# A fourth raw-weight buffer, stores held back by one weight, and four columns begun on half of their tokens

## The chip, the cores and the metric

The kernel runs on one core of a Trainium2 chip. The metric is device time in microseconds (us) of one execution, the median of several runs; lower is better.

## What is computed

Attention with a memory term, then two feed-forward networks (FFNs), in float32 (B=4, H=8, S=576, D=64, model width 512, inner width 2048):

```
a = softmax(causal(q k^T / 8));  local = a v
mem = (phi(q) M_prev) / (phi(q) z_prev + 1e-6);  g = sigmoid(beta)
x = g * mem + (1 - g) * local          # 4 x 576 tokens x 512
x = softplus(x W1in) W1out             # first FFN ("layer 0")
x = elu(x W2in) W2out                  # second FFN ("layer 1")
```

The weights arrive as float64, viewed as pairs of 32-bit words.

## The kernel before

**Tokens.** The 2304 tokens are cut into five chunks (`CHUNKS`). Chunk 0 is tokens 0 to 255 of batches 0 and 1, so its 512 columns are batch 0's half (columns 0 to 255, `CA` = 256) and batch 1's half. Each chunk goes through layer 0 and then layer 1.

**Weights.** A weight tile is 128x4x128: `0i3` is column block 3 of layer 0's input matrix, `1o2_1` is piece 1 of output block 2 of layer 1. Every matrix has 16 such tiles. The first time, a tile is loaded raw (512 KB, `raw`, into a buffer of the tag `big`), turned into float32 on ACT and DVE (`convert`: L606 on ACT, L607 and L608 on DVE), and split into a high part (L97 on ACT) and a low part (L618 on DVE) in one of the four `w` buffers of the pool `wp`. It is also stored to a scratch tensor in DRAM (`save`, L583, 512 KB), from which the later chunks reload it (L656). The tag `big` has three buffers, which the attention's raw head tiles (`load_head`) share. All loads and stores of weights go through SP's queue, which is in order: a store that waits for its conversion holds up the load behind it.

**FFN.** A column block `f` of an input product is 12 matmuls into one PSUM bank `h`: for each of four k blocks (128 of the 512 inputs, two heads' pair of the attention) high x high, high x low and low x high (L690 to L692). Then come the activation and a split into `g` (L665 to L696, on ACT and DVE), which free the bank. There are four `h` banks (`psf`), and the early attention of batches 0 and 1 uses the same four for its scores (L371, `bank`). An output product has 16 pieces of 12 matmuls (L707 to L709).

**Attention.** The early part ("A") of batches 0 and 1 runs first. `gather_pair` writes one k block of `x` for one batch (L150, L151); its last matmul is kept in `marks`. The rest (A of batches 2 and 3, then the late part "B" of all four batches) is cut into steps, which `order` in `TUNE` mixes into the FFN: an entry `(chunk, layer, a, b)` means `a` steps for each of the 16 column blocks and `b` steps for each of the 16 output pieces.

**Order.** A scheduler sets each engine's order when the program is built; each engine then works in order. Fourteen of the first matrix's 16 tiles are converted before chunk 0 starts. So in layer 1 of chunk 0 (184 to 310 us of the span, below "the w2i stage" and "the w2o stage") every weight is loaded raw, converted, used and stored for the first time.

Of the kernel before, what the change touches and what calls it, by code (L numbers as in the profile page):

```python
# [8 lines left out]
F32 = mybir.dt.float32  # L9
# [4 lines left out]
I32 = mybir.dt.int32  # L14
# [3 lines left out]
NP = H // 2  # L18
KD = DM // 128
# [6 lines left out]
CA = 256  # L26
# [13 lines left out]
    hi='ssss ssss', lo='v', sc='vv ssv',  # L40


    order=((0, 0, 0.95, 0.95), (0, 1, 0.25, 1.0), (1, 0, 0.45, 1.6), (1, 1, 0.4, 0.9), (2, 0, 0.3, 0.8), (2, 1, 0.4, 0.7), (3, 0, 0.3, 0.8), (3, 1, 0.4, 0.7), (4, 0, 0.0, 0.0), (4, 1, 0.0, 0.0)),
)


# [12 lines left out]
def kernel(  # L59
# [20 lines left out]
    four = ctx.enter_context(tc.tile_pool(name="four", bufs=4))  # L80
    tri = ctx.enter_context(tc.tile_pool(name="tri", bufs=3))
    wp = ctx.enter_context(tc.tile_pool(name="wp", bufs=4))
    gp = ctx.enter_context(tc.tile_pool(name="gp", bufs=KF))
    dram = ctx.enter_context(tc.tile_pool(name="dram", bufs=1, space=bass.MemoryType.DRAM))
    psf = ctx.enter_context(tc.tile_pool(name="psf", bufs=4, space=bass.MemoryType.PSUM))
# [49 lines left out]
    def x(c, k):  # L135
        return slots[SLOT[c]][k]
# [5 lines left out]
    gates, column, marks = [], [], {}  # L142
# [11 lines left out]
    def attention(b, part, pool, early=None):  # L154
# [15 lines left out]
        def own(h):  # L170
            return slice(64 * h, 64 * h + 64)
# [12 lines left out]
            d["kq", p] = t  # L184

        def load_head(n):
            t = tri.tile([128, 960], F32, name="qk", tag="big")
            if n % 2:
                at = S + QO[4]
                ge.dma_start(t[:, 0:at], qk[b, n, :, 0:at])  # L190
                ge.dma_start(t[:, at:at + 64], qk[b, n, :, at + 64:at + 128])
                ge.dma_start(t[:, at + 64:at + 128], qk[b, n, :, at:at + 64])
            else:
                ge.dma_start(t, qk[b, n, :, 0:960])
            d["qk", n] = t
# [169 lines left out]
        def scores_pair(n):  # L365
            p, ps = n // 2, [bank(n), bank(n + 1)]
            for i in (1, 0):
                w_, at = width(i), poff(0, i)
                for h in range(2):
                    t, q0 = d["kq", p], CA + 128 * i  # L370
                    te.matmul(ps[h][:, at:at + w_], t[own(h), q0:q0 + 128], t[own(h), 0:w_], start=True, stop=True)  # L371
            for h in range(2):
                P, neg = sph[h], d["neg", n + h]
                for i in (1, 0):
                    w_, at, to = width(i), poff(0, i), poff(n, i)
                    negmax(P[:, to:to + w_], ps[h][:, at:at + w_], mask[:, 512 - w_:512], neg[:, i:i + 1])
                    expo(n + h, i)
# [213 lines left out]
            fetched[key] = raw(w1i[f])  # L591

    def raw(src):
        w64 = tri.tile([128, 4, 128, 2], I32, name="w64", tag="big")
        load = nc.sync.dma_start(w64.rearrange("p k n t -> p (k n t)"), src.bitcast(I32))
        raw_loads.append(load.ins)
        sync.append(load.ins)
        return w64

    def convert(src, key, w=None):  # L600
        wr = tri.tile([128, 4, 128], F32, name="wr", tag="wr")
        if wide:
            w64 = fetched.pop(key) if key in fetched else raw(src)
            low, high = w64[:, :, :, 0], w64[:, :, :, 1]
            wi = wr.bitcast(I32)
            se.activation(wr, high.bitcast(F32), ACTF.Prelu, scale=2.0 ** -112, alpha=-(2.0 ** 32))  # L606
            ve.tensor_scalar(wi, wi, 3, None, ALU.logical_shift_left)  # L607
            ve.scalar_tensor_tensor(wi, low, 29, wi, ALU.logical_shift_right, ALU.bitwise_or)  # L608
        else:
            w64 = tri.tile([128, 4, 128, 2], I32, name="w64", tag="big")  # L610
            load = nc.sync.dma_start(wr.rearrange("p k n -> p (k n)"), src)
            raw_loads.append(load.ins)
            sync.append(load.ins)
        if w is None:
            w = w64.rearrange("p k n t -> p (k n t)").rearrange("p (s k n) -> p s k n", s=2, k=4).bitcast(F32R)
        hi, lo = w[:, 0], w[:, 1]
        copy(E[T["hi"].split()["o" in key][int(key[0])]], hi, wr)
        E[T["lo"]].tensor_sub(lo, wr, f32(hi))  # L618
        return w
# [3 lines left out]
    def weights(src, key):  # L623
        if key in made:
            w = made.pop(key)
            unsaved.append((key, w))
        else:
            early = key.startswith("0i") and key not in scratch
            with tc.high_priority(offset=T["pri"][key in scratch]), tc.issue_after(softs[int(key[2:]) - 10]) if early else nullcontext():
                new = key not in scratch  # L630
                passes[key] = passes.get(key, 0) + 1
                w = make(src, key)
            if len(raw_loads) >= KF:
                with tc.issue_after(sync[-1]):
                    while unsaved:
                        save(*unsaved.pop(0))
            with tc.issue_after(sync[-1]):
                put()
            if new and not (key in twice and passes[key] == 1):
                unsaved.append((key, w))  # L640
        return w[:, 0], w[:, 1]
# [11 lines left out]
    def make(src, key, pool=None):  # L653
        w = (pool or wp).tile([128, 2, 4, 128], F32R, name="w", tag="g" if pool else "w")
        if key in scratch:
            sync.append(nc.sync.dma_start(f32(w), scratch[key]).ins)  # L656
        else:
            convert(src, key, w)
        return w
# [3 lines left out]
    def act(c, layer, f, t, h):  # L663
# [9 lines left out]
        else:  # L673
            ve.tensor_scalar(t, h, 0.0, None, ALU.min)
            se.activation(t, t, ACTF.Exp)
            ve.scalar_tensor_tensor(t, t, -1.0, h, ALU.add, ALU.max)  # L676

    def ffn(c, layer):
        win, wout = ((w1i, w1o), (w2i, w2o))[layer]
        N = WIDTH[c]  # L680
        gs = []
        for f in range(KF):
            hi, lo = weights(win[f], f"{layer}i{f}")
            t = two.tile([128, 512], F32, name="t", tag="t")
            g = gp.tile([128, 2, 512], F32R, name="g", tag="g")
            h = psf.tile([128, 512], F32, name="h", tag="h")
            with tc.issue_after(marks[1, NP - 1][0]) if (c, layer) == (0, 0) and f < 4 else nullcontext():
                for k in range(KD):
                    xk = x(c, k)
                    te.matmul(h[:, :N], hi[:, k, :], xk[:, 0, :N], start=k == 0, stop=False)  # L690
                    te.matmul(h[:, :N], hi[:, k, :], xk[:, 1, :N], start=False, stop=False)  # L691
                    end = te.matmul(h[:, :N], lo[:, k, :], xk[:, 0, :N], start=False, stop=k == KD - 1)  # L692
            column[:] = [end.ins]
            act(c, layer, f, t[:, :N], h[:, :N])
            se.copy(g[:, 0, :N], t[:, :N])  # L695
            ve.tensor_sub(g[:, 1, :N], t[:, :N], f32(g)[:, 0, :N])  # L696
            gs.append(g)
            if layer and f == KF - 1:
                busy[c].add("in")
            yield  # L700
        for d in range(KD):
            h = psf.tile([128, 512], F32, name="h", tag="h")
            for u in range(4):
                hi, lo = weights(wout[d, u], f"{layer}o{d}_{u}")
                for k in range(4):
                    f = 4 * u + k
                    te.matmul(h[:, :N], hi[:, k, :], gs[f][:, 0, :N], start=f == 0, stop=False)  # L707
                    te.matmul(h[:, :N], hi[:, k, :], gs[f][:, 1, :N], start=False, stop=False)  # L708
                    end = te.matmul(h[:, :N], lo[:, k, :], gs[f][:, 0, :N], start=False, stop=f == KF - 1)  # L709
                column[:] = [end.ins]  # L710
                if u < 3:
                    yield
            if layer == 0:
                y = x(c, d)
                se.copy(y[:, 0, :N], h[:, :N])
                ve.tensor_sub(y[:, 1, :N], h[:, :N], f32(y)[:, 0, :N])
            else:
                o = two.tile([128, 512], F32, name="t", tag="t")
                copy(se, o[:, :N], h[:, :N])
                outs.append((c, d, o))  # L720
                if c == len(CHUNKS) - 1:
                    put()
            yield
# [36 lines left out]
    with tc.tile_pool(name="pre", bufs=1) as pre, tc.tile_pool(name="pre3", bufs=2) as pre3:  # L760
# [12 lines left out]
        with tc.issue_after(marks[1, NP - 2][1]), tc.issue_after(marks[1, NP - 2][2]):  # L773
            while len(made) < count:
                key = f"0i{len(made)}"
                made[key] = make(w1i[len(made)], key)
    late = ctx.enter_context(tc.tile_pool(name="late", bufs=1))
    slots.append([late.tile([128, 2, WIDTH[2]], F32R, name=f"x2_{k}") for k in range(KD)])

# [100 lines left out]
```

## Time and profile before

| | us |
|---|---|
| median of 3 runs (1055.76 to 1058.61) | 1056.13 |
| the profiled execution | 1053.93 |
| its span, first to last instruction | 1052.1 |

The profile is of one execution, so its parts add up to the span and not to the median. PE is TensorE's matmuls, PEld its weight loads, DVE is VectorE, ACT is ScalarE, SP issues the weight transfers, POOL the attention's. An engine's row shows when an instruction began, how long it took and, in brackets, how long the engine had stood before it and what released it.

### The profile page before, as it was taken

The page shows a single profiled execution, that of the slowest core. Times are in us where ns is not written, and L with a number is a line of the kernel's source. Part 1 is how long each engine was busy: PE and PEld are TensorE (multiplying, and loading weights), DVE is VectorE, ACT ScalarE, POOL GpSimd, SP SyncE. Part 2 cuts the span into 40 slices and gives each one's busy share as a digit, 9 for nine tenths or more (in the row PEclk, how much of TensorE's full clock was granted, in tenths as well). Part 3 has the DMA queues.
Part 4 walks back from the last instruction along what each step waited for, and adds up shares of the span by engine and source line. Part 5 has one row for each costly group of instructions (what it writes and reads, how often), then busy time and mean ns, then how long its engine had stood idle before and what let it go on. Part 6 is the DMA issues. An engine that isn't in the chain of part 4 may idle for free.

```text
span 1052.1 us, 15858 instructions
## 1 busy us (share of the span) xinstructions
PE 1011.3 (96%) x5249; PEld 897.7 (85%) x5249; DVE 672.3 (64%) x1701; ACT 664.5 (63%) x1518; POOL 104.0 (10%) x198
## 2 busy tenths in 40 slices
PE   6699999978989999999999999999999999999998
PEld 4477777767868888888889899999999999999998
DVE  6958887887768665798666667854665570240640
ACT  5869865877669955787679756555885440570420
POOL 7121221020111011000110011000000000000000
PEclk9899999999999999999999999999999999999999
DMA  8558888975786466566775666666755567777675
GB/s 245 166 207 311 288 293 299 336 264 197 232 288 223 160 203 203 177 221 227 259 245 184 223 221 215 191 233 213 234 189 172 175 233 243 251 235 233 235 238 171
DMA packets 71185, 240.27 MB, mean 228 GB/s; under 512 B 10288, under 2 KB 15552, under 8 KB 71104
## 3 DMA queue, kind: packets, MB, share of 16 engines
q1 hardware_dynamic: 62272, 207.65, 58.2%
q0 software_dynamic: 8832, 31.61, 9.8%
q8 instruction: 42, 0.69, 0.3%
q14 instruction: 39, 0.32, 0.1%
HBM read 200.95 MB, written 38.27 MB: 227 GB/s over the span
## 4 chain that ended last, share of the span: by engine, by line
PE 77%; DVE 8%; DMA 6%; ACT 5%; issue 3%; SPq 0%; ACTq 0%; DVEq 0%
PE h L707 12%; PE h L709 12%; PE h L708 12%; PE h L690 10%; PE h L692 10%; PE h L691 10%; DMA w<-in_w2o 3%; PE tp L409 3%; PE o L456 2%; PE s L343 2%; DMA w<-in_w2i 1%; PE s L355 1%; DVE wr L608 1%; DVE w L618 1%; DVE sph L332 1%
## 5 line engine op out<-in xcount | busy, mean ns | idle before, releaser
L690 PE MATMUL h<-x,w 128*128 128x512 f32 (+2 forms) x640 | 240.7, 378 | 8.3 <-DVE t L672 7.4
L707 PE MATMUL h<-g,w 128*128 128x512 f32 (+2 forms) x640 | 241.7, 378 | 0.3 <-ACT w L97 0.2
L709 PE MATMUL h<-g,w 128*128 128x512 f32 (+2 forms) x640 | 239.2, 374 | 0.5 <-DVE w L618 0.5
L708 PE MATMUL h<-g,w 128*128 128x512 f32 (+2 forms) x640 | 238.9, 373 | 0.0
L692 PE MATMUL h<-x,w 128*128 128x512 f32 (+2 forms) x640 | 238.3, 373 | 0.0
L691 PE MATMUL h<-x,w 128*128 128x512 f32 (+2 forms) x640 | 238.3, 373 | 0.0
L690 PEld LDWEIGHTS h<-x,w 128*128 128x128 f32 x640 | 120.9, 189 | 24.5 <-DVE t L672 9.4
L709 PEld LDWEIGHTS h<-g,w 128*128 128x128 f32 x640 | 121.2, 189 | 13.2 <-DVE w L618 1.1
L707 PEld LDWEIGHTS h<-g,w 128*128 128x128 f32 x640 | 121.2, 189 | 13.1 <-ACT w L97 0.7
L692 PEld LDWEIGHTS h<-x,w 128*128 128x128 f32 x640 | 120.7, 189 | 13.7 <-issue 0.2
L691 PEld LDWEIGHTS h<-x,w 128*128 128x128 f32 x640 | 121.0, 189 | 12.0
L708 PEld LDWEIGHTS h<-g,w 128*128 128x128 f32 x640 | 121.3, 190 | 10.9
L696 DVE TENSOR_TENSOR g<-t,g 128x512 fp32r<-128x512 f32 (+2 forms) x160 | 100.9, 634 | 32.2 <-ACT g L695 30.6
L695 ACT CAST g<-t 128x512 fp32r<-128x512 f32 (+2 forms) x160 | 91.5, 574 | 33.2 <-DVE t L676 25.8
L336 ACT ACTIVATE sph<-sph,neg 128x256 f32<-128x256 f32 (+4 forms) x144 | 83.4, 580 | 32.2 <-DVE neg L332 32.0
L668 DVE SCALAR_TENSOR_TENSOR t<-h,t 128x512 f32<-128x512 f32 (+2 forms) x80 | 50.3, 635 | 65.0 <-ACT t L667 64.6
L332 DVE CUSTOM_DVE_ANT_0 sph<-s,mask 128x256 f32<-128x256 f32 (+3 forms) x112 | 56.0, 520 | 49.4 <-PE s L343 41.9
L606 ACT ACTIVATE wr<-w 128x512 f32<-128x512 f32 x70 | 46.7, 672 | 36.9 <-DMA w<-in_w2o 16.3
L409 PE MATMUL tp<-ident,sph 128*128 128x128 f32 x400 | 61.6, 278 | 8.3 <-DVE sph L385 3.6
L409 PEld LDWEIGHTS tp<-ident,sph 128*128 128x128 f32 x400 | 48.9, 144 | 16.1 <-DVE sph L385 3.9
L420 DVE TENSOR_TENSOR ptj<-tp,ptj 128x512 fp32r<-128x512 f32 (+2 forms) x80 | 40.1, 513 | 31.8 <-ACT ptj L419 25.2
L97 ACT COPY t<-h 128x512 f32<-128x512 f32 (+2 forms) x20 | 10.8, 542 | 74.4 <-PE h L709 74.3
(134 smaller groups left out, 1498.8 us busy)
## 6 DMA issues: line engine op xcount, KB each, us to landing
w<-s_0i SPq DMA_DIRECT2D x64, 512.0 KB, 4.2
w<-s_0o SPq DMA_DIRECT2D x64, 512.0 KB, 3.3
w<-s_1i SPq DMA_DIRECT2D x62, 512.0 KB, 3.5
w<-s_1o SPq DMA_DIRECT2D x60, 512.0 KB, 4.1
w<-in_w2o SPq DMA_DIRECT2D x20, 512.0 KB, 4.6
w<-in_w2i SPq DMA_DIRECT2D x18, 512.0 KB, 5.5
w<-in_w1i SPq DMA_DIRECT2D x16, 512.0 KB, 4.9
s_0i<-w SPq DMA_DIRECT2D x16, 512.0 KB, 10.5
```

The source lines that it names most:

```text
L332: ve.tensor_tensor_reduce(out=dst, in0=ps, in1=m, scale=-0.125, scalar=least, op0=ALU.add, op1=ALU.min, accum_out=acc)
L336: se.activation(Pi, Pi, ACTF.Exp, scale=-1.0, bias=d["neg", n][:, i:i + 1], accum_out=sums(n, i))
L409: te.transpose(pt, sph[n % 2][:, poff(n, i) + 128 * j:poff(n, i) + 128 * j + 128], ident)
L668: ve.scalar_tensor_tensor(t, h, 0.0, t, ALU.max, ALU.add)
L690: te.matmul(h[:, :N], hi[:, k, :], xk[:, 0, :N], start=k == 0, stop=False)
L691: te.matmul(h[:, :N], hi[:, k, :], xk[:, 1, :N], start=False, stop=False)
L692: end = te.matmul(h[:, :N], lo[:, k, :], xk[:, 0, :N], start=False, stop=k == KD - 1)
L695: se.copy(g[:, 0, :N], t[:, :N])
L696: ve.tensor_sub(g[:, 1, :N], t[:, :N], f32(g)[:, 0, :N])
L707: te.matmul(h[:, :N], hi[:, k, :], gs[f][:, 0, :N], start=f == 0, stop=False)
L708: te.matmul(h[:, :N], hi[:, k, :], gs[f][:, 1, :N], start=False, stop=False)
L709: end = te.matmul(h[:, :N], lo[:, k, :], gs[f][:, 0, :N], start=False, stop=f == KF - 1)
```

## The change

Four edits. The tag `big` moves to a pool of its own with four buffers. While layer 1's weights are first converted, `weights` leaves one tile unsaved, so that each store is issued one weight later. The steps of attention per FFN piece are shifted: chunk 0's layer 0 takes 32 steps instead of 30.4, the output pieces of its layer 1 take 12 instead of 16, and those of chunk 1's layer 0 take 28 instead of 25.6. And `open_columns` begins column blocks 0 to 3 of chunk 0 on batch 0's half and the first two k blocks, behind batch 1's last scores and batch 0's third gather; `ffn` later does the other half of these k blocks.

```diff
-    order=((0, 0, 0.95, 0.95), (0, 1, 0.25, 1.0), (1, 0, 0.45, 1.6), ...
+    order=((0, 0, 1.0, 1.0), (0, 1, 0.25, 0.75), (1, 0, 0.45, 1.75), ...
...
+    big = ctx.enter_context(tc.tile_pool(name="big", bufs=4))
...
-            t = tri.tile([128, 960], F32, name="qk", tag="big")
+            t = big.tile([128, 960], F32, name="qk", tag="big")
...
-                    te.matmul(ps[h][:, at:at + w_], t[own(h), q0:q0 + 128], t[own(h), 0:w_], start=True, stop=True)
+                    done = te.matmul(ps[h][:, at:at + w_], t[own(h), q0:q0 + 128], t[own(h), 0:w_], start=True, stop=True).ins
+            marks[b, p, "s"] = done
...
-        w64 = tri.tile([128, 4, 128, 2], I32, name="w64", tag="big")
+        w64 = big.tile([128, 4, 128, 2], I32, name="w64", tag="big")
...
-                    while unsaved:
+                    while len(unsaved) > (new and key[0] == "1"):
                         save(*unsaved.pop(0))
...
+    def product(h, hi, lo, c, k, a, z):
+        xk = x(c, k)
+        te.matmul(h[:, a:z], hi[:, k, :], xk[:, 0, a:z], start=k == a == 0, stop=False)
+        te.matmul(h[:, a:z], hi[:, k, :], xk[:, 1, a:z], start=False, stop=False)
+        return te.matmul(h[:, a:z], lo[:, k, :], xk[:, 0, a:z], start=False, stop=k == KD - 1)
+
+    starts = {}
+
+    def open_columns():
+        for f in range(4):
+            starts[f] = (*weights(w1i[f], f"0i{f}"), psf.tile([128, 512], F32, name="h", tag="h"))
+        for k, behind in enumerate((marks[1, NP - 1, "s"], marks[0, 2][0])):
+            with tc.high_priority(offset=2000), tc.issue_after(behind):
+                for hi, lo, h in starts.values():
+                    product(h, hi, lo, 0, k, 0, CA)
+
     def ffn(c, layer):
...
-            hi, lo = weights(win[f], f"{layer}i{f}")
+            begun = (c, layer) == (0, 0) and f in starts
+            hi, lo = starts[f][:2] if begun else weights(win[f], f"{layer}i{f}")
...
-            h = psf.tile([128, 512], F32, name="h", tag="h")
-            with tc.issue_after(marks[1, NP - 1][0]) if (c, layer) == (0, 0) and f < 4 else nullcontext():
+            h = starts[f][2] if begun else psf.tile([128, 512], F32, name="h", tag="h")
+            with tc.issue_after(marks[1, NP - 1][0]) if begun else nullcontext():
                 for k in range(KD):
-                    xk = x(c, k)
-                    te.matmul(h[:, :N], hi[:, k, :], xk[:, 0, :N], start=k == 0, stop=False)
-                    te.matmul(h[:, :N], hi[:, k, :], xk[:, 1, :N], start=False, stop=False)
-                    end = te.matmul(h[:, :N], lo[:, k, :], xk[:, 0, :N], start=False, stop=k == KD - 1)
+                    end = product(h, hi, lo, c, k, CA if begun and k < 2 else 0, N)
...
+        open_columns()
```

PE's order behind batch 0's third gather (`o_400`, pair 2), before. `tp_467` is the memory product of the next pair.

```order
L472 MATMUL o_400<-ident_89,e_263 128x128 x2
L475 MATMUL o_400<-pt_346,ar0_2_147 64x256
L475 MATMUL o_400<-pt_347,ar0_2_147 64x256
L475 MATMUL o_400<-pt_346,ar0_2_147 64x128
L475 MATMUL o_400<-pt_347,ar0_2_147 64x128
L287 MATMUL tp_467<-mz_421,phi_443 128x130 x2
```

The same place now (the gather is `o_403`; `h_768` and `h_769` are column blocks 0 and 1, `x0_0` and `x0_1` the first two k blocks).

```order
L477 MATMUL o_403<-pt_349,ar0_2_150 64x128
L477 MATMUL o_403<-pt_350,ar0_2_150 64x128
L682 MATMUL h_768<-x0_0_100,w_209 128x256
L683 MATMUL h_768<-x0_0_100,w_209 128x256
L684 MATMUL h_768<-x0_0_100,w_209 128x256
L682 MATMUL h_768<-x0_1_101,w_209 128x256
L683 MATMUL h_768<-x0_1_101,w_209 128x256
L684 MATMUL h_768<-x0_1_101,w_209 128x256
L682 MATMUL h_769<-x0_0_100,w_250 128x256
L683 MATMUL h_769<-x0_0_100,w_250 128x256
L684 MATMUL h_769<-x0_0_100,w_250 128x256
```

With block 1's three for the second k block, which follow, twelve matmuls of 256 columns stand between the gather and the next memory product (`tp_470` now). Blocks 2 and 3 stand in the same way behind batch 0's fourth gather.

SP's order at the beginning of layer 1's output matrix, before. `w64_2653` is the raw tile of `1o0_2`, whose converted tile is `w_2651`.

```order
L595 DMA w64_2653<-in_w2o 128x1024
L583 DMA s_1o0_0_2624<-w_2541 128x1024
L595 DMA w64_2688<-in_w2o 128x1024
L595 DMA w64_2738<-in_w2o 128x1024
L583 DMA s_1o0_2_2695<-w_2651 128x1024
L583 DMA s_1o0_3_2745<-w_2686 128x1024
L595 DMA w64_2795<-in_w2o 128x1024
L583 DMA s_1o1_0_2802<-w_2736 128x1024
L595 DMA w64_2838<-in_w2o 128x1024
```

The same place now. The raw tile of `1o0_2` is `w64_2692`, its converted tile `w_2690`.

```order
L597 DMA w64_2692<-in_w2o 128x1024
L585 DMA s_1i14_2662<-w_2556 128x1024
L597 DMA w64_2737<-in_w2o 128x1024
L585 DMA s_1o0_0_2744<-w_2632 128x1024
L597 DMA w64_2795<-in_w2o 128x1024
L597 DMA w64_2820<-in_w2o 128x1024
L585 DMA s_1o0_2_2802<-w_2690 128x1024
L597 DMA w64_2863<-in_w2o 128x1024
L585 DMA s_1o0_3_2827<-w_2735 128x1024
```

The store of `1o0_2` stands behind two later loads before and behind three now, that of `1o0_3` behind one before and three now.

## Rows read from the trace of the kernel before

**Rows 1.** The page: the span, and PE's busy time.

```profile
span 1052.1 us, 15858 instructions
...
PE 1011.3 (96%) x5249; PEld 897.7 (85%) x5249; DVE 672.3 (64%) x1701; ACT 664.5 (63%) x1518; POOL 104.0 (10%) x198
```

**Rows 2.** Windows: busy us by engine, granted clock, DMA share, GB/s.

```profile
0.00:60.00 60.00, 41.64 (x215) 30.39 (x215) 45.28 (x190) 40.91 (x125) 24.25 (x52) 0.94 0.62 183
60.00:184.00 124.00, 122.65 (x610) 95.36 (x611) 99.49 (x281) 93.63 (x219) 25.49 (x46) 1.00 0.84 295
184.00:235.00 51.00, 43.58 (x186) 33.72 (x185) 42.62 (x78) 41.39 (x76) 6.48 (x12) 0.97 0.85 299
235.00:310.00 75.00, 67.41 (x330) 55.34 (x329) 58.46 (x145) 51.59 (x118) 9.15 (x18) 0.95 0.70 236
310.00:1000.00 690.00, 688.24 (x3661) 635.59 (x3660) 415.63 (x989) 427.84 (x965) 38.63 (x70) 1.00 0.65 216
```

**Rows 3.** PE's timeline at the stalls of both stages.

```profile
212.13 0.50 PE L690 MATMUL h<-x,w 128*128 128x512 f32 x1 [2.65 <-DVE t L672]
...
212.93 0.39 PE L690 MATMUL h<-x,w 128*128 128x512 f32 x1
...
217.60 0.40 PE L692 MATMUL h<-x,w 128*128 128x512 f32 x1
...
228.03 0.80 PE L690 MATMUL h<-x,w 128*128 128x512 f32 x1 [3.97 <-DVE t L672]
...
231.15 0.40 PE L691 MATMUL h<-x,w 128*128 128x512 f32 x1
...
263.57 0.66 PE L409 MATMUL tp<-ident,sph 128*128 128x128 f32 x4 [3.25 <-DVE ptj L420]
...
265.23 0.80 PE L707 MATMUL h<-g,w 128*128 128x512 f32 x1 [0.21 <-ACT w L97]
...
268.74 0.40 PE L709 MATMUL h<-g,w 128*128 128x512 f32 x1
...
294.29 0.77 PE L409 MATMUL tp<-ident,sph 128*128 128x128 f32 x5 [3.62 <-DVE sph L385]
```

**Rows 4.** ACT's timeline ahead of PE's stall that ends at 228.03.

```profile
217.97 0.99 ACT L97 CAST R<-qk 128x960 fp32r<-128x960 f32 x1 [1.42 <-DMA qk<-in_qk]
...
222.97 0.67 ACT L606 ACTIVATE wr<-w 128x512 f32<-128x512 f32 x1 [1.39 <-DMA w<-in_w2o]
```

**Rows 5.** ACT's longest wait, 184 to 310: us in total, times, longest.

```profile
ACT wr L606 <- DMA w<-in_w2o: 11.3, 11, 1.5
```

**Rows 6.** SP's waits, 184 to 310: us in total, times, longest.

```profile
SPq L595 <- DVE wr L608: 28.8, 15, 3.4
SPq L583 <- DVE w L618: 23.9, 15, 4.1
```

**Rows 7.** Landing times of w2o's 16 loads, by tile.

```profile
DMA to landing us min/median/max: 3.4/4.6/5.9
```

**Rows 8.** Landing times of 14 of the stores of w2i, by tile.

```profile
DMA to landing us min/median/max: 3.3/4.8/7.4
```

**Rows 9.** PE's timeline in the early attention, after two of batch 0's gathers.

```profile
45.08 0.69 PE L287 MATMUL tp<-mz,phi 128*128 128x130 f32 x4 [1.46 <-issue]
...
49.43 0.68 PE L287 MATMUL tp<-mz,phi 128*128 128x130 f32 x4 [1.42 <-DVE phi L263]
```

**Rows 10.** DVE's timeline: the last reads of two score banks.

```profile
44.24 0.29 DVE L332 CUSTOM_DVE_ANT_0 sph<-h,mask 128x128 f32<-128x128 f32 x1
...
48.65 0.29 DVE L332 CUSTOM_DVE_ANT_0 sph<-h,mask 128x128 f32<-128x128 f32 x1
```

**Rows 11.** PE's timeline: two matmuls of 256 columns, and the next.

```profile
282.21 0.39 PE L458 MATMUL o<-ptl,vs 128*128 128x256 f32 x2
282.45 0.33 PE L459 MATMUL o<-sph,vs 128*128 128x64 f32 x2
```

**Rows 12.** The page: the weight loads of L690, mean ns of one.

```profile
L690 PEld LDWEIGHTS h<-x,w 128*128 128x128 f32 x640 | 120.9, 189 | 24.5 <-DVE t L672 9.4
```

More of the change, by code (lines that the diff above doesn't have):

```diff
@@ L40 @@
     hi='ssss ssss', lo='v', sc='vv ssv',
-    order=((0, 0, 0.95, 0.95), (0, 1, 0.25, 1.0), (1, 0, 0.45, 1.6), (1, 1, 0.4, 0.9), (2, 0, 0.3, 0.8), (2, 1, 0.4, 0.7), (3, 0, 0.3, 0.8), (3, 1, 0.4, 0.7), (4, 0, 0.0, 0.0), (4, 1, 0.0, 0.0)),
+    order=((0, 0, 1.0, 1.0), (0, 1, 0.25, 0.75), (1, 0, 0.45, 1.75), (1, 1, 0.4, 0.9), (2, 0, 0.3, 0.8), (2, 1, 0.4, 0.7), (3, 0, 0.3, 0.8), (3, 1, 0.4, 0.7), (4, 0, 0.0, 0.0), (4, 1, 0.0, 0.0)),
 )
@@ L609, in convert @@
         else:
-            w64 = tri.tile([128, 4, 128, 2], I32, name="w64", tag="big")
+            w64 = big.tile([128, 4, 128, 2], I32, name="w64", tag="big")
             load = nc.sync.dma_start(wr.rearrange("p k n -> p (k n)"), src)
```

## The prediction

> **What bounds the kernel now.** I read the page's first part, then windows over the whole span, then PE's timeline where the windows show PE standing, then the waits of ACT and SP in that stretch. PE is busy 1011.3 of 1052.1 us [rows 1], so time can only come from the 40.8 us in which PE stands, from matmuls that run at the lower clock, or from fewer matmul columns. The windows say where PE stands: 18.4 us in the first 60 us, 1.4 us up to 184, 7.4 us in the w2i stage, 7.6 us in the w2o stage, 1.8 us in the 690 us after that, and the rest at the end [rows 2]. Nothing in the change touches the last two.
>
> In the two stages the granted clock is 0.97 and 0.95 as well [rows 2]. PE's timeline shows how: after standing 3.97 us it goes on at 228.03, and the seven matmuls up to 231.15 take 3.12 us. At the full level the twenty steps from 212.93 to 217.60 take 4.67 us, 0.233 each, so seven are 1.63 us, and 1.5 us were lost at the lower of the two levels (1.2 instead of 2.4 GHz). The eight from 265.23 to 268.74 take 3.51 us instead of 1.87, after 3.25 us of standing: 1.6 lost. The stall of 3.62 us that ends at 294.29 has the same tail [rows 3]; I take 1.6 there too. After 2.65 us of standing, at 212.13, the clock stays up [rows 3]. So the w2i stage holds 7.4 + 1.5 = 8.9 us and the w2o stage 7.6 + 3.2 = 10.8 us that better feeding could give back.
>
> What ends these stalls is named as DVE, but DVE and ACT were late themselves. Ahead of the stall that ends at 228.03 ACT stood 1.42 us for a raw head tile and 1.39 us for a raw weight [rows 4], with the activations that free PE's banks queued behind. In both stages ACT stands 11.3 us in 11 places for raw w2o tiles [rows 5]. These loads are late because SP is in order: it stands 28.8 us at a load until DVE has read a raw buffer, and 23.9 us at a store until DVE has finished a conversion [rows 6]. A load lands 4.6 us after its issue in the median [rows 7]; it was asked for too late rather than served slowly.
>
> **The early columns.** Twenty-four matmuls of 512 columns (four column blocks, two k blocks, three products) become 24 of 256 in the early attention and 24 of 256 behind it. No row shows this shape on FFN tiles. The nearest is the gather's 256-column matmul: two take 282.45 - 282.21 = 0.24 us, 0.12 each, plus what their predecessor hides, so 0.117 is half of a 512-column step and fits [rows 11]. What is left behind the attention falls by 24 x (0.233 - 0.117) = 2.8 us. If instead the 189 ns of a weight load [rows 12] set the spacing, it would be 24 x (0.233 - 0.189) = 1.1 us; the load of a 256-column matmul has the same shape, so I stay with 2.8. The Trainium skill ("TensorE: Matmul & The Clock Gate", section "LDWEIGHTS") gives a load its columns over 1.2, 107 ns for 128; an estimate by it leaves the 2.8 as it is, and the trace's 189 ns disagree with it.
>
> In the early part these matmuls stand ahead of the attention's chain. Blocks 0 and 1 come where PE stood 1.46 us before 45.08 [rows 9]. Their banks are free when DVE has read the scores, the second at 44.24 + 0.29 = 44.53 [rows 10]. Six matmuls of 0.117 behind that, and some of block 0 still ahead of them, end near 45.4: the chain slips 0.3 us. Blocks 2 and 3 come in the 1.42 us before 49.43; the second bank is free at 48.94, and they end near 49.8: 0.35 us. At half clock (the window shows 0.94 in this stretch) the twelve take 2.8 instead of 1.4 us and the slip is about 1.7 and 1.8, of which later waits of the chain take some. I take 0.5 us in all, so the early columns are worth 2.3, between a loss of 0.7 (2.8 - 3.5) and 2.8. At the weight load's price the low end is -2.4.
>
> **Fourth buffer and later stores.** They remove no instruction; each load stands one store earlier in SP's queue. Counted in the order, a first store of an output tile of layer 1 stands behind 2.5 later loads in the mean instead of 1.4 (12 stores; of an input tile behind 4.5 instead of 4.1, 14 stores). Conversion and load of a tile are a loop: with one load between, a tile can be asked for only when its predecessor's conversion is done; with two, when that of the tile before it is done. A w2o piece now takes about 75 / 16 = 4.7 us [rows 2], as long as the median load; one piece more of lead covers ACT's 11.3 us of standing, none longer than 1.5. In the w2o stage transfers are busy 0.70 of the time, so there is room for it; DVE and ACT are busy 58 and 52 of 75 us [rows 2].
>
> In the w2i stage the room is smaller: DVE is busy 42.6 and ACT 41.4 of 51 us, and transfers 0.85 [rows 2]. Without its 8.9 us the stage would be 42.1 us long, less than DVE's work in it. So at most about half comes back unless work moves out, and the order shows only a little doing so. I take 4.4, between 0 and 8.9. A loss is not excluded; it is the rival on the slower side.
>
> **The shift of steps.** All 83.2 steps up to chunk 1's second layer remain, so PE's work is the same. The w2o stage loses a quarter of its attention (84 matmuls in the order instead of 118), and with it DVE's and ACT's side work. The steps go where PE never stands: 1.6 into chunk 0's layer 0, 2.4 into chunk 1's layer 0 (PE busy 122.7 of 124 and 688 of 690 us, DVE 99.5 and 416 [rows 2]). Cover: if DVE were full there, 4 steps of some 1.8 us would come back as PE waits, 7 us; at 80% and 60% it isn't. The two stalls of the w2o stage wait for attention tiles (`ptj`, `sph` [rows 3]), so thinning it acts on the same 10.8 us as the earlier loads. For both together I take 7.5, between 0 and 10.8: two stalls of over 3 us should shrink to less than the one of 2.65 us, behind which the clock stayed up; that returns their 3.2 us of slow matmuls and half or more of their 7.6.
>
> **Sum.** 2.3 + 4.4 + 7.5 = 14.2 us. The profiled execution takes 1053.93, 2.2 less than the median of 1056.13, so the same difference on the median gives 1041.9; I say 1042.
>
> **The rivals.** *Transfers bound the w2i stage.* At 0.85 busy and 299 GB/s over 51 us [rows 2], a load that is issued sooner only stands longer on the same transfer engines. Then that term is 0 and the sum 9.8: 1046. Against it: ACT's waits are in places, not throughout. The Trainium skill ("DMA: Bandwidth & Descriptors", section "Issuing engines are not separate DMA queues") says that transfers run on the same 16 engines whoever issues them; the 0.85 agrees with that, and by this rule the rival is right wherever the share is near 1.
>
> *The stalls are bursts of attention work.* If ACT and DVE are late because a step brings many operations at once, loads that come earlier change only which operation waits. Then the early columns alone remain: 2.3, 1054, no difference that this kernel's measurement can tell (0.3%, 3.2 us). For it: the stalls end on `ptj` and `sph`, not on weights. Against it: the 11.3 us of ACT.
>
> *Late stores hold the converted buffers* (slower). A `w` buffer may be written again only when its store has landed, and the store now stands directly ahead of the load of the tile that wants the buffer. That tile's high part is written about 2 us after its load has landed (L606, L607, L608 and their handovers). So it decides where a store takes over 2 us longer than the load behind it. Stores land in 4.8 us in the median and 7.4 at most [rows 8], loads in 3.4 at least [rows 7]; the worst pair costs 7.4 - 3.4 - 2 = 2 us, in ACT's queue, ahead of activations. If 7 of the 26 stores of layer 1 did that and nothing else came back but 2.3, it is 1056.1 + 14 - 2.3 = 1068.
>
> *Everything comes back*: 2.8 + 8.9 + 10.8 = 22.5, 1034.
>
> **How the numbers follow.** Forecast 0.55 (its own range 1036 to 1048), transfer bound 0.17, bursts 0.13, late stores 0.08, everything 0.07. Of the forecast and the transfer bound all is faster, of the bursts about half lie within 0.3%, and the bounds below zero take a little: faster 0.80, same 0.11, slower 0.09. A range from 1035 to 1053 leaves out the late stores, most of the bursts and the far end of the last case, some 0.2.
>
> **What would show it.** Right: ACT's waits for raw w2o tiles fall from 11.3 to below 4 us; no stall over 3 us between 184 and 310, and a granted clock of 1.00 there; PE begins the attention's next memory products less than 1 us later and FFN work 2 us sooner. Wrong: ACT waiting at the high part (L97) for stores; DVE above 95% in the w2i stage with PE standing as before; a new wait in chunk 0's first layer, where the steps have gone; or the early matmuls spaced 0.19 or 0.23 us apart.

## The result, and the profile after

The change is faster: 1044.74 us in the median of 4 runs (1043.49 to 1046.74), against 1055.95 of 4 runs of the kernel before (1054.19 to 1058.61). The ratio is 0.9896, with a 95% interval from 0.9871 to 0.9921, so 11.2 us came back where 14.2 were forecast. The profiled execution took 1046.74, the slowest of the four; its early attention ran late (batch 0's third gather at 43.31 us, against 40.75 to 41.97 in the three other profiled kernels with the early columns), and that of the kernel before was 2 us below its median, so the two profiles differ by only 7.2 us.

The page and the windows of the changed kernel answer to [rows 1, 2].

```profile
span 1044.7 us, 15881 instructions
...
PE 1013.4 (97%) x5273; PEld 899.7 (86%) x5273; DVE 670.4 (64%) x1701; ACT 664.9 (64%) x1518; POOL 101.9 (10%) x198
```

```profile
0.00:60.00 60.00, 45.00 (x229) 34.69 (x230) 45.14 (x190) 40.62 (x123) 23.61 (x52) 0.91 0.66 191
60.00:184.00 124.00, 120.99 (x627) 94.82 (x625) 100.83 (x286) 95.27 (x224) 25.71 (x47) 1.00 0.84 297
184.00:235.00 51.00, 47.02 (x205) 35.12 (x204) 45.57 (x87) 42.53 (x79) 7.68 (x16) 1.00 0.88 313
235.00:310.00 75.00, 74.02 (x368) 61.80 (x367) 58.00 (x139) 56.64 (x125) 9.10 (x17) 1.00 0.77 273
310.00:1000.00 690.00, 685.65 (x3636) 633.05 (x3635) 415.21 (x993) 424.06 (x958) 35.79 (x67) 1.00 0.63 212
```

In the w2o stage PE now stands 1.0 us instead of 7.6, with a granted clock of 1.00. In the w2i stage it still stands 4.0 us, also at 1.00. Two windows got worse: PE stands 3.0 instead of 1.4 us between 60 and 184, and 4.3 instead of 1.8 us behind 310.

The table below is worked out from PE's timelines: the time from the first FFN matmul of a product to that of the next, and in brackets the attention's matmuls that begin between them (each product has 192 of its own). "c1" is chunk 1, "0" and "1" are the layers.

| kernel | ratio to before | w2i | w2o | c1 0 in | c1 0 out | c1 1 in |
|---|---|---|---|---|---|---|
| before | 1 | 57.1 (22) | 72.4 (121) | 53.1 (62) | 59.7 (118) | 60.4 (105) |
| the change | 0.9896 | 55.2 (31) | 55.2 (82) | 56.2 (73) | 58.6 (108) | 67.7 (120) |
| columns alone | 0.9993 | 57.5 (22) | 70.0 (121) | 54.7 (62) | 59.7 (118) | 59.7 (105) |
| shift alone | 1.0062 | 55.8 (28) | 70.5 (94) | 52.8 (61) | 58.6 (108) | 70.3 (136) |
| stores alone | 1.0041 | 56.9 (22) | 76.8 (121) | 55.0 (62) | 59.7 (118) | 60.2 (105) |
| buffer alone | 0.9866 | 55.0 (22) | 55.9 (86) | 57.3 (97) | 59.7 (118) | 63.7 (115) |
| buffer and stores | 0.9890 | 55.2 (22) | 56.9 (86) | 60.2 (97) | 58.1 (106) | 59.9 (108) |
| the change without columns | 0.9925 | 55.8 (31) | 56.0 (82) | 55.5 (73) | 58.6 (108) | 68.6 (120) |
| the change without shift | 0.9891 | 55.3 (22) | 57.4 (86) | 61.0 (97) | 58.1 (106) | 59.7 (108) |
| buffer, half of the shift | 0.9879 | 56.2 (31) | 57.1 (82) | 57.0 (87) | 59.7 (118) | 63.2 (106) |
| heads' own buffer | 0.9859 | 51.3 (22) | 56.3 (86) | 62.2 (97) | 59.8 (118) | 60.0 (106) |
| buffer, w2i thinned | 0.9828 | 51.7 (6) | 58.0 (94) | 58.3 (101) | 58.5 (107) | 61.1 (111) |

The w2o stage became 17.2 us shorter. The 10.8 us of standing and slow matmuls are gone from it; the rest is attention, 39 matmuls fewer, which turn up later. The second input product of chunk 1 became 7.3 us longer.

ACT's and SP's waits from 184 to 310 us answer to [rows 5, 6], the landing times of w2o's loads to [rows 7]. The columns are total, times and longest.

```profile
ACT wr L608 <- DMA w<-in_w2o: 9.5, 9, 2.0
```

```profile
SPq L597 <- DVE wr L610: 28.2, 16, 4.5
SPq L585 <- DVE w L620: 17.6, 11, 4.7
```

```profile
DMA to landing us min/median/max: 3.4/5.1/7.8
```

ACT waits nearly as long for raw tiles as before, and SP as long for raw buffers; only PE in the w2o stage no longer waits.

### The profile page after: what moved, and what is told of

Its sections match the earlier page's. It is cut to its first block, busy times and chain, and to the rows that moved or that the text cites. A ratio compares the mean times of both kernels' runs of the same rounds, so it can differ in the third digit from the quotient of the medians.

```text
span 1044.7 us, 15881 instructions
## 1 busy us (share of the span) xinstructions
PE 1013.4 (97%) x5273; PEld 899.7 (86%) x5273; DVE 670.4 (64%) x1701; ACT 664.9 (64%) x1518; POOL 101.9 (10%) x198
## 4 chain that ended last, share of the span: by engine, by line
PE 82%; ACT 6%; DVE 4%; DMA 4%; issue 2%; SPq 0%; POOL 0%; ACTq 0%; DVEq 0%
PE h L723 13%; PE h L725 13%; PE h L724 12%; PE h L682 10%; PE h L684 10%; PE h L683 10%; PE tp L411 3%; PE o L458 2%; PE s L344 2%; DMA w<-in_w1i 2%; PE s L356 1%; PE o L477 1%; PE s L372 1%; DVE wr L610 1%; DMA out_t<-t 1%
## 5 line engine op out<-in xcount | busy, mean ns | idle before, releaser
L682 PE MATMUL h<-x,w 128*128 128x416 f32 (+3 forms) x648 | 242.9, 377 | 8.4 <-DVE t L674 4.0
L683 PE MATMUL h<-x,w 128*128 128x416 f32 (+3 forms) x648 | 240.5, 371 | 0.0
L684 PE MATMUL h<-x,w 128*128 128x416 f32 (+3 forms) x648 | 240.3, 371 | 0.0
L682 PEld LDWEIGHTS h<-x,w 128*128 128x128 f32 x648 | 122.5, 189 | 27.6 <-DVE t L674 7.1
L684 PEld LDWEIGHTS h<-x,w 128*128 128x128 f32 x648 | 122.4, 189 | 13.9 <-DVE w L620 0.6
L683 PEld LDWEIGHTS h<-x,w 128*128 128x128 f32 x648 | 122.6, 189 | 11.8
L667 ACT ACTIVATE t<-h 128x512 f32<-128x512 f32 (+2 forms) x80 | 44.2, 552 | 20.1 <-PE h L684 8.9
```

The costliest lines, as they stand in the source:

```text
L682: te.matmul(h[:, a:z], hi[:, k, :], xk[:, 0, a:z], start=k == a == 0, stop=False)
L683: te.matmul(h[:, a:z], hi[:, k, :], xk[:, 1, a:z], start=False, stop=False)
L684: return te.matmul(h[:, a:z], lo[:, k, :], xk[:, 0, a:z], start=False, stop=k == KD - 1)
```

## The experiments

Each ratio is to the kernel before, run beside it on the same chip, with its 95% interval. The edits are against the changed kernel unless said otherwise.

**Early columns alone.** The old steps, stores and three buffers.

```diff
-    order=((0, 0, 1.0, 1.0), (0, 1, 0.25, 0.75), (1, 0, 0.45, 1.75), ...
+    order=((0, 0, 0.95, 0.95), (0, 1, 0.25, 1.0), (1, 0, 0.45, 1.6), ...
-    big = ctx.enter_context(tc.tile_pool(name="big", bufs=4))
+    big = ctx.enter_context(tc.tile_pool(name="big", bufs=3))
-                    while len(unsaved) > (new and key[0] == "1"):
+                    while unsaved:
```

> Only the early columns; three raw buffers, stores and steps as before. Forecast: 24 matmuls of half width leave the path behind the early attention, 2.8 us less a slip of 0.5, so 2.3 us off, 1053.7 on a median of 1056; the trace of the whole change gives 3.1 us from batch 0's third gather to the first output product. The early matmuls are spaced 0.12 us. Rival (a slip of the attention's chain eats it): same time as before, and the last early gather more than 2 us later behind the third one than the 18.9 us of before.

It took 1054.88 us, 0.9993 (0.9975 to 1.0011): no difference that can be told, and 2.3 us were expected.

**Buffer and later stores**: the old steps and no early columns.

```diff
-        open_columns()
```

> Fourth raw buffer and later stores; steps as before, no early columns. Theory of late loads: ACT's wait for raw w2o tiles between 184 and 310 us falls from 11.3 to below 4 us, the stalls of 3.97, 3.25 and 3.62 us shrink below 2.65 with no slow matmuls behind them, and 8 to 10 us come back: 1047. Rival (bursts of attention work): loads come earlier, but stalls that end on ptj and sph stay over 3 us each, and it is 1054 or more.

1043.9 us, 0.9890 (0.9873 to 0.9907), more than was expected; a second measurement, below, gave 0.9885. ACT still waits 7.6 us for raw w2o tiles, and one stall of 2.78 us is left, in the w2i stage.

**Shift of steps alone**: the kernel before with the new `order`.

> Only the shift of attention steps. Theory of late loads: ACT still waits some 10 us for raw w2o tiles, one stall of over 3 us stays, and at most 3 us come back: 1053. Rival (bursts of attention work): the two stalls of the w2o stage go without any help of the loads, 7 us or more come back: 1049 or less.

1061.85 us, 1.0062 (1.0045 to 1.0079): slower by 6 us, which neither theory expected. Chunk 1's second input product became 9.9 us longer. The w2o stage became 1.9 us shorter with 27 attention matmuls fewer, but PE stands 8.7 us in it, and the two long stalls now end on weights (L97 writes a tile's high part):

```profile
256.58 0.80 PE L707 MATMUL h<-g,w 128*128 128x512 f32 x1 [4.89 <-ACT w L97]
...
294.47 0.50 PE L707 MATMUL h<-g,w 128*128 128x512 f32 x1 [2.54 <-ACT w L97]
```

**Without the early columns**: only the call of `open_columns` is left out.

> The whole change but the early columns. If the terms add up, it takes 3 us more than the whole change: 1047.5 against 1044.7; the w2i and w2o stages look as in the whole change, with no stall over 1 us and a granted clock of 1.00. If the early columns also paid elsewhere (by where chunk 0 then stands against the loads), the difference is 5 us or more.

1047.46 us, 0.9925 (0.9906 to 0.9945), as expected where the terms add up.

**Without the shift**: only the `order` line as in the first experiment.

> The whole change with the steps of before: fourth buffer, later stores and early columns. If the terms add up as measured (0.989 for buffer and stores, 0.999 for the columns), ratio 0.988, 1043. Rival (the columns pay more where the loads keep up, as the 2.7 us between the change with and without them suggest): 0.986 or less, 1041. In both it beats the change, whose shift of steps cost 3 us or more; chunk 1's second input product takes 60 us again instead of 68.

1044.52 us, 0.9891 (0.9867 to 0.9915): beside the columns the shift is worth nothing that can be told, though a gain of some 2 us or more was expected from leaving it out. Chunk 1's second input product takes 59.7 us again, but its first 61.0 instead of 56.2: the attention only stands elsewhere.

**Buffer and later stores, once more**, beside the last.

> The same kernel as buffer_and_stores, on the chip of without_order: 0.989 again. The difference between the two is what the early columns are worth: below 1 us if the first activations, which begin no earlier, decide when chunk 0's first product goes on; 2 to 3 us if PE's work behind the attention decides.

1042.78 us, 0.9885 (0.9856 to 0.9915): without the shift the columns are worth nothing that can be told.

**Fourth buffer alone**: the old steps, `while unsaved:`, no early columns.

> Four raw buffers, stores as early as before, steps as before, no columns. In the order the first stores of w2o tiles stand behind 2.3 later loads in the mean (2.4 with later stores, 1.4 before). If the lead of a load over its store decides, nearly all of the gain is here: 0.990, 1045. Rival (the store ahead holds the load up anyway): 0.995 or more, and ACT still waits 8 us or more for raw w2o tiles.

1041.84 us, 0.9866 (0.9839 to 0.9893): one edit gives as much as the whole change or more (0.9896; the intervals overlap). Its windows of the two stages:

```profile
184.00:235.00 51.00, 46.13 (x199) 35.55 (x199) 46.16 (x85) 43.56 (x82) 7.40 (x14) 0.97 0.90 314
235.00:310.00 75.00, 75.00 (x379) 63.07 (x378) 60.16 (x150) 60.47 (x134) 10.18 (x19) 1.00 0.80 272
```

PE doesn't stand at all in the w2o stage, with the steps of before. The attention there still fell from 121 to 86 matmuls: the order on PE is made when the program is built, and with another buffer it came out differently. The stores of w2o tiles also stand behind more loads, 2.4 in the mean instead of 1.4.

**Later stores alone**: the old steps, three buffers, no early columns.

> Later stores with three raw buffers, steps as before, no columns. In the order the first stores of w2o tiles stand behind 2.1 later loads in the mean, those of w2i tiles behind 4.1 as before. If the lead decides, the w2o stage gains 5 us or more and the w2i stage nothing: 0.995, 1050. Rival (late stores hold the converted buffers): ACT waits at the high part (L97) for stores, and the time is that of before or more.

1060.83 us, 1.0041 (1.0024 to 1.0058): slower by some 4 us, where 5 us less were expected of a longer lead. The waits of ACT and SP in the two stages, the window of the w2o stage and its two long stalls:

```profile
ACT wr L608 <- DMA w<-in_w2o: 17.7, 10, 2.8
```

```profile
SPq L597 <- DVE wr L610: 41.4, 15, 7.1
SPq L585 <- DVE w L620: 13.6, 10, 3.0
```

```profile
235.00:310.00 75.00, 64.44 (x307) 52.70 (x306) 56.58 (x142) 50.14 (x114) 8.91 (x18) 0.93 0.66 218
```

```profile
264.91 1.12 PE L411 MATMUL tp<-ident,sph 128*128 128x128 f32 x4 [3.91 <-DVE ptj L422]
...
298.41 0.80 PE L723 MATMUL h<-g,w 128*128 128x512 f32 x1 [4.46 <-ACT w L98]
```

SP's standing moved from the stores (23.9 to 13.6 us) to the loads (28.8 to 41.4 [rows 6]). A load that stands ahead of a store isn't sooner where it waits for DVE to free a raw buffer; and the store, now behind that wait, leaves later.

**A buffer of the heads' own**: three for the raw weights and one for attention's raw heads; everything else as in the fourth buffer alone.

```diff
-    big = ctx.enter_context(tc.tile_pool(name="big", bufs=4))
+    big = ctx.enter_context(tc.tile_pool(name="big", bufs=3))
+    head = ctx.enter_context(tc.tile_pool(name="head", bufs=1))
-            t = big.tile([128, 960], F32, name="qk", tag="big")
+            t = head.tile([128, 960], F32, name="qk", tag="head")
```

> Still four large buffers, no later stores, no columns, steps as before; but three are for raw weights alone and one for the attention's raw head tiles alone. If the fourth buffer pays because heads no longer take one from the weights, it is as fast as four shared ones: 0.987, 1042. If the weights need four, or the heads two at a time (ACT waits longer at R for a head tile), it is between that and before: 0.993 or more, 1048.

1040.83 us, 0.9859 (0.9839 to 0.9879). The order changed with it: the stores of w2o tiles stand behind 4.2 later loads in the mean, against 2.4 with four shared buffers.

**w2i thinned**: the fourth buffer alone, with 2.4 of the 4 steps of the w2i stage moved to the output pieces behind it.

```diff
-    order=((0, 0, 0.95, 0.95), (0, 1, 0.25, 1.0), ...
+    order=((0, 0, 0.95, 0.95), (0, 1, 0.1, 1.15), ...
```

> Four shared buffers alone, and the attention steps of chunk 0's second layer moved from its input product (1.6 instead of 4 steps) to its output product (18.4 instead of 16). With four buffers PE no longer stands in the output product, and the 4.8 us of stalls left in the input product come behind ACT's waits for raw head tiles. If those are bursts of attention, they go: 0.983, 1038. If conversion and activation alone fill DVE there (9.2 of 10 us busy), they stay and the output product only gets longer: 0.987 or more.

1038.0 us, 0.9828 (0.9806 to 0.9851): the lowest ratio of all, though its interval overlaps those of the buffer alone and of the heads' own buffer. The change, measured beside it, has 0.9904 (0.9882 to 0.9927). The windows of the two stages:

```profile
184.00:235.00 51.00, 45.93 (x202) 35.52 (x201) 44.51 (x79) 43.63 (x81) 4.86 (x9) 1.00 0.91 319
235.00:310.00 75.00, 74.28 (x376) 61.97 (x375) 58.59 (x145) 57.03 (x126) 12.34 (x24) 1.00 0.80 273
```

The time is the one expected if the stalls go, but they didn't: PE stands 5.1 us in the w2i stage's window, and 4.9 with the buffer alone.

**The change once more**, beside the last two.

> The whole change again, on the chip of the two others: 0.9896. If the fourth buffer is what pays and the other edits cost about 3 us, it is slower than both others of this call unless one of them fails.

1044.99 us; its chunk 1 second input product took 66.3 us.

**Fourth buffer and half of the shift**: chunk 1's share of the shift left out.

```diff
-    order=((0, 0, 0.95, 0.95), (0, 1, 0.25, 1.0), (1, 0, 0.45, 1.6), ...
+    order=((0, 0, 1.0, 1.0), (0, 1, 0.25, 0.9), (1, 0, 0.45, 1.6), ...
```

> The kernel with only the fourth buffer, and half of the shift: the 1.6 steps that chunk 0's layer 0 takes more come out of the output pieces of its layer 1 (0.9 for each instead of 1.0), and chunk 1's layer 0 keeps its 25.6. Theory one, that the shift costs in chunk 1, where its 2.4 further steps bring a burst of attention ahead of layer 1's input product: that product takes 60 to 64 us as with the fourth buffer alone, without a stall of over 1 us near 433 us, and the whole is within 2 us of the fourth buffer alone, 0.986 to 0.989 of the kernel before. Theory two, that any shift out of the output pieces costs, since with the fourth buffer PE no longer stands there: that product takes 66 to 70 us as in the whole change, and the ratio is 0.990 to 0.993.

1043.63 us, 0.9879 (0.9856 to 0.9903), and 63.2 us in the product in question, as with the buffer alone: the first theory's numbers, though the interval reaches into the second's. Its other sign failed narrowly: PE still has stalls of over 1 us in that product, the nearest at 438.35.

```profile
438.35 0.39 PE L460 MATMUL o<-ptl,vs 128*128 128x256 f32 x1 [1.01 <-ACT ptl L421]
...
470.58 0.41 PE L458 MATMUL o<-ptj,vs 128*128 128x320 f32 x1 [2.00 <-ACT ptj L421]
```

## Why the forecast held, and where its steps failed

The time is within the range and 2.7 us from the forecast (1044.7 against 1042). That they are so close is partly luck: of its three terms one was too small (w2o), one about right (w2i) and one nearly absent (the columns), and a cost was missing. What the two stages gave back above the forecast (15.7 against 11.9 us of standing and slow matmuls) made up in part for the columns and that cost.

**w2o: more than forecast, and by another cause.** The forecast took 7.5 of the 10.8 us for the fourth buffer, the later stores and the shift together, and laid it on the lead of a load over the stores in SP's queue. All 10.8 came, and the buffer alone brings them (its window of the w2o stage has PE busy 75.00 of 75 us at a granted clock of 1.00). It isn't that the w2o stage holds less attention now (82 or 86 matmuls instead of 121): with the shift alone it holds 94, and PE stands 8.7 us there, for weights. Nor is it the lead by itself. Later stores raise the lead with three buffers too (2.2 later loads ahead of a store of w2o, counted as before, instead of 1.4), and they cost 4 us there; on top of the buffer they make no difference that can be told (0.9890 and 0.9885 against 0.9866, intervals that overlap). So "with two loads between" failed as a rule of the queue: what pays is the fourth large buffer. As it raises the lead as well (2.4), no run shows whether it would pay without that. One buffer for the heads does as much (0.9859): with heads out of the way, three for weights are enough. That fits a bound through sharing, but the longer lead of that kernel (4.2) came with it, so the sharing is not shown by itself. Five were not tried.

The marker failed too: ACT's waits for raw tiles were to fall below 4 us and are at 9.5, and at 6.4 with the buffer alone, while in the window of the w2o stage PE stands 1.0 us (for a reload, behind the last piece) and not at all. Waits of an off-path engine, added up, told nothing of PE; in place of the sum, the single waits behind which PE's operands are queued have to be looked up. Of the other signs, two came: no stall of over 3 us between 184 and 310 us, and a granted clock of 1.00 there.

**w2i: the size came, the reason is not shown.** The forecast took 4.4 of 8.9 us, because DVE would be nearly full. Standing fell from 7.4 to 4.0 us and the slow matmuls are gone, so 4.9 came back; the stage is only 1.9 us shorter, as 9 more attention matmuls run in it. But DVE was not full: it is busy 45.6 of 51 us with the change. And half is no bound: with the heads' own buffer the stage is 51.3 us, 5.8 less than before with the same 22 attention matmuls.

The rival of the bursts is not shown either. In the kernel with only the buffer the longest stall goes back to a late raw head:

```profile
209.22 1.00 ACT L98 CAST R<-qk 128x960 fp32r<-128x960 f32 x1 [2.22 <-DMA qk<-in_qk]
...
210.24 0.76 DVE L239 TENSOR_TENSOR R<-qk,R 64x576 fp32r<-64x576 f32 x1 [1.60 <-ACT R L98]
...
214.76 0.69 DVE L674 SCALAR_TENSOR_TENSOR t<-t,h 128x512 f32<-128x512 f32 x1
...
215.51 0.50 PE L682 MATMUL h<-x,w 128*128 128x512 f32 x1 [2.58 <-DVE t L674]
```

ACT stands for the head and DVE for ACT; from 210.24 DVE works without a pause, on the head, conversions and the FFN, until the operation that frees PE's bank comes at 214.76. So a late head and a full DVE make this stall together. Thinning took 16 of the 22 attention matmuls out, and PE stands as long as without that. The 3.3 us by which the stage became shorter are some 1.8 us of those matmuls and 1.5 us of slow ones (granted clock 1.00 instead of 0.97 over 51 us). That its time came out as for the bursts is luck, and what sets the standing that is left in the w2i stage stays open.

**Early columns: right at the place, given back next door.** After the first few the 24 matmuls run 0.12 us apart, so the 189 ns of a weight load [rows 12] don't set the spacing, and PE goes on with the attention's next memory product right behind them:

```profile
47.36 0.28 PE L683 MATMUL h<-x,w 128*128 128x256 f32 x1
47.48 0.28 PE L684 MATMUL h<-x,w 128*128 128x256 f32 x1
47.59 0.61 PE L288 MATMUL tp<-mz,phi 128*128 128x130 f32 x4
```

From the third to the eighth gather it takes 19.26 us, and 19.23 without the columns: no slip, where 0.5 us was forecast (with three buffers and the old steps it is 21.10 instead of 19.70, a slip whose cause I didn't follow). But from the eighth gather to the end of the first input product it takes 56.38 instead of 57.12 us: 0.7 us of the 2.8. Most of the rest is standing, 1.65 us, in the timelines of the change:

```profile
74.11 0.50 PE L682 MATMUL h<-x,w 128*128 128x512 f32 x1 [1.65 <-DVE t L670]
```

```profile
70.17 0.60 ACT L667 ACTIVATE t<-h 128x512 f32<-128x512 f32 x1 [1.87 <-PE h L684]
70.67 0.61 ACT L98 CAST w<-wr 128x512 fp32r<-128x512 f32 x1
71.17 0.60 ACT L667 ACTIVATE t<-h 128x512 f32<-128x512 f32 x1
71.66 1.15 ACT L668 ACTIVATE t<-t 128x512 f32<-128x512 f32 x2
72.70 1.15 ACT L669 ACTIVATE t<-t 128x512 f32<-128x512 f32 x2
...
73.36 1.29 DVE L670 SCALAR_TENSOR_TENSOR t<-h,t 128x512 f32<-128x512 f32 x2 [1.36 <-ACT t L669]
```

All four banks are full, and the fifth column block needs the first one back. PE runs the four blocks side by side, so the first of them ends only at about 70.1, 2.4 us before PE has done the last (74.11 - 1.65 = 72.46). From there ACT takes two blocks together through three activations, and DVE's read behind them frees the bank 4 us later. The forecast counted PE's matmuls and left out that chain; the same 1.65 us of standing is in all four profiled kernels with the columns. It is the new wait in chunk 0's first layer that the forecast named as a sign of being wrong, though not by the steps. Why the columns gain 2 to 3 us beside the shift (0.9896 and 0.9904 against 0.9925) and none without it stays open; the intervals overlap.

**Shift of steps: the missing cost.** The forecast sent 2.4 steps into "chunk 1's layer 0", where PE never stands and DVE is at 60%, at no cost. They don't run there. In the table, chunk 1's first output product has 108 attention matmuls instead of 118, and its second input product 136 (shift alone) or 120 (the change) instead of 105. As the order on PE is made when the program is built, this could be counted beforehand. There the change stands, and its clock falls behind it:

```profile
433.56 0.66 PE L411 MATMUL tp<-ident,sph 128*128 128x128 f32 x4 [1.66 <-DVE ptj L422]
435.27 0.41 PE L454 MATMUL o<-phi,ms 128*128 128x320 f32 x1 [1.05 <-DVE phi L307]
435.88 1.09 PE L411 MATMUL tp<-ident,sph 128*128 128x128 f32 x4 [0.20 <-DVE phi L308]
436.75 0.79 PE L682 MATMUL h<-x,w 128*128 128x512 f32 x1
...
442.25 0.46 PE L684 MATMUL h<-x,w 128*128 128x512 f32 x1
```

```profile
430.00:440.00 10.00, 7.07 (x30) 5.09 (x30) 9.56 (x23) 9.05 (x22) 0.00 (x0) 0.78 0.63 222
440.00:450.00 10.00, 10.00 (x45) 8.33 (x45) 8.30 (x21) 5.83 (x14) 2.39 (x5) 0.88 0.93 327
```

DVE is busy 9.56 and ACT 9.05 of the first 10 us: the condition that the forecast named ("if DVE were full there") is met, in a window of 10 us that the mean over 690 us hides. The lower clock costs some 3 us more (0.22 and 0.12 of 10 us each). A full DVE alone is not enough, and so the cause is argued and not shown: in the kernel before it is as full from 450 to 460 us, and PE does not stand.

```profile
450.00:460.00 10.00, 10.00 (x52) 8.48 (x51) 9.54 (x25) 6.23 (x15) 0.54 (x1) 1.00 0.82 293
```

The price with three buffers is 6 us in all, with buffer and stores some 3.7 (0.9925 against 0.9890, intervals that just touch), and beside the columns not measurable. Part of the 7.3 us in the product is only attention that left another one. The single edits don't add: by their ratios -14.1, +4.3, +6.5 and -0.7 would be -4.0, not -11.2; later stores cost nothing that can be told once there is a fourth buffer, and the shift less.

**The other rivals.** Transfers did not bound the w2i stage: thinned, it runs them at 0.91 and 319 GB/s, above the 0.85 and 299 of before, and is shorter. So 0.85 still left room. The Trainium skill ("DMA: Bandwidth & Descriptors", section "Issuing engines are not separate DMA queues") has all transfers run on the same 16 engines, whichever engine starts them. The profile's share is over 16 engines too, and no run here tests the rule. Late stores are not seen to hold the converted buffers: no wait of ACT at the high part for a store is among the change's waits in the two stages, nor among those of the later stores alone, though that kernel was slower as this rival has it.

## What to carry to other kernels

Where several streams share a ring of staging buffers, count the buffers before reordering the queue that fills them: with too few, an earlier place in the queue only moves the wait from the store to the load. Work that is brought forward on one engine is worth what the next engine in the chain can take up, so follow the resource (here a PSUM bank) to where it comes free. When steps are moved, look up in the new order where they land, and read the load there in windows of 10 us, not of a stage.

## What the runs showed of the hardware that was not expected

- Landing times didn't follow the rate. w2o's loads land in 5.1 us in the median with the change, while the w2o stage moves 273 GB/s, and in 4.5 us with the buffer alone, at 272; before they land in 4.6 at 236 GB/s [rows 2, 7], and with later stores alone in 4.9 at 218. What sets them stays open.
- The clock can fall some time after a stall. With the buffer alone, PE stood 2.58 us before 215.51 and went on at 0.23 us a step; 1.7 us later, without another gap, the steps took 0.43 (granted clock 0.50 from 217.0 to 220.2, the lower level), and by 220.41 they took 0.23 again (1.00 from 220.2 to 222):

```profile
216.30 0.39 PE L682 MATMUL h<-x,w 128*128 128x512 f32 x1
...
217.18 0.63 PE L682 MATMUL h<-x,w 128*128 128x512 f32 x1
217.61 0.63 PE L683 MATMUL h<-x,w 128*128 128x512 f32 x1
...
220.41 0.39 PE L684 MATMUL h<-x,w 128*128 128x512 f32 x1
```

  So reading only the matmuls right behind a stall can miss what it costs. Where the forecast read them, at 212.13 behind 2.65 us [rows 3], twenty steps at full speed followed, so it cost nothing there; and with the heads' own buffer PE stood 2.49 us before 213.21 and the granted clock stayed at 1.00 to 225. The length of a stall alone does not tell.
